# First feed-forward product of six blocks as one Strassen level over 64-row, 128-column products

## The chip, the cores and the metric

The kernel runs on one core of a Trainium2 chip. A core has a matrix engine (TensorE, in the profile PE, with its weight loads shown apart as PEld), a vector engine (VectorE, DVE), an activation engine (ScalarE, ACT), a general engine (GpSimd, POOL) and a queue that issues transfers (SyncE, SP). Each works through its own instructions in their written order and waits on semaphores where it needs another's result. Matrix products end in PSUM, eight banks of 128 partitions x 512 words of 32 bits; everything else stands in SBUF, 128 partitions wide. The metric is the time of one execution on the device, in microseconds (us).

## What is computed

One transformer block on 2048 tokens of 576 features, all inputs in bfloat16. A is linear attention with 32 heads, B the feed-forward part with 4608 hidden features:

```python
mod = (silu(c) @ w_mod).reshape(c.shape[0], 6, 1, -1)
sa, ca, ga, sb, cb, gb = (mod[:, i].copy() for i in range(6))
h = _layernorm(x, axis=-1) * (1 + ca) + sa
x = x + ga * _A_ref(h, A_wqkv, A_w_phi, A_wo)
h = _layernorm(x, axis=-1) * (1 + cb) + sb
x = x + gb * _B_ref(h, B_w1, B_w2)

def _B_ref(x, w1, w2):
    h = jnp.einsum('bsd,df->bsf', x, w1)
    h = jnp.maximum(h, 0)
    return jnp.einsum('bsf,fd->bsd', h, w2)
```

The change is in the first product of B, x @ w1 followed by the maximum with 0.

## The kernel before

**Stages.** The 2048 tokens are 16 tiles of 128 (`NT`), the feed-forward part works on pairs of tiles, eight blocks (`NB`). A first phase, to about 92 us, loads everything, works out the modulation vectors and the keys, values and queries, and sums the key-value matrix. Its order is written out by hand, word by word, in `ORDER`; every word calls one entry of `JOBS`. Some words matter here: `sK` sums exponentials (VectorE, `sums`, L283, into `Rk`), `rK` inverts the sums by a logarithm and an exponential (ScalarE, `k_r`, L300 and L301, into `rk`), `pA` scales them (GpSimd, L594, into `Ak`), `pM` forms a ratio (GpSimd, L599, into `rat`) and multiplies with it (L290). `vE` scales the values with `Ak` (VectorE, L304). `ga` and `gb` are two gate rows: they leave PSUM as quarters into `gt` (`row_e`, L366), go to a buffer in DRAM (`row_w`, L369, one DMA each, `gatd<-gt`) and come back spread over all partitions (`row_r`, L372). `wo` scales the output weights with the first gate row (GpSimd, L632), `xp` scales two tiles of x (GpSimd, L507). Each of `gt`, `Rk`, `rk`, `Ak`, `rat`, `sc`, `mask`, `epsr` and `zero` is an SBUF tile of its own.

**Blocks.** After that, `l1` and `l2` run in turn for each block. `l1(b)` is the first product: the 256 tokens of the block are the moving operand, a 64 x 128 piece of w1 the stationary one. Features come in nine chunks of 64 (`NS`), hidden features in 36 groups of 128. The layout puts the lower half of the hidden features in partitions 0 to 63 and the upper half in 64 to 127, and h2 holds the features in both halves, so two matmuls (`hf` 0 and 1) of 64 rows and 256 columns work in the two halves of the array at the same time. `l1` has nine units `u` of two groups each; a unit fills two banks, and `relu` empties them with two ScalarE instructions (L691 and L692) and one or two of VectorE (L693, and L708 in every third unit) into A11, U3, A12, A22 and U2 in fp16.

`l2(b)` is the second product, by a Strassen scheme of seven products already (Winograd's form): `prod` runs 18 matmuls of 128 x 288 each (L730), with results in banks X, Y and Z, and `fin` adds gates and the residual (VectorE L715 or L717, GpSimd L718 and L719, with `yt` as buffer). The hooks `in_l1` and `in_l2` place the work for later tiles among the matmuls: residual and second layernorm of the next block in `in_l1` (`add_res` L412, `bn` L239 and L240, `ln2_rs` L415 and L416, `ln2_apply` L421, a DMA transpose into h2 at L402) and one query tile in units 5 and 6 (`q_next`: VectorE sums L283, GpSimd L345 and L290, then a DMA transpose into ET at L349); the attention of later tiles (`attend`, L390 with L397 and L398), its transposes (`o_turn`) and the scaling of h2 (`h_scale`, L827) in `in_l2`. `project` (L798 and L805, banks 6, 7, 0 and 1) follows `l2` for blocks 1 to 6, so before the first products of blocks 2 to 7, but not before block 8's.

What the program's engines wait for is put in by the tile framework: it orders any two accesses to the same SBUF or PSUM region of which one writes. The order of the instructions on each engine is the written one (`manual_schedule`).

```python
pe.matmul(PS[:, 2 * u + hf, n * 256 + o:n * 256 + o + w], lhsT=w1[b0:b0 + 64, c, j * P:(j + 1) * P],
          rhs=hb[b0:b0 + 64, c, o:o + w], start=(n == 0 and c == 0 and tile != 0), stop=False,
          skip_group_check=True)
```

Of the kernel before, what the change touches and what calls it, by code (L numbers as in the profile page):

```python
# [60 lines left out]

@with_exitstack
def tile_block(ctx, tc, a, out):
# [51 lines left out]
    mask = small([P, KVW], BF16, "mask")  # L115
    epsr = small([1, KVW + P], BF16, "epsr")
# [18 lines left out]
    sc = small([P, 4, NX], BF16, "sc")  # L135
    Rk = small([P, 4, 2 * H], FP32, "Rk")
    rk = small([P, 4, 2 * H], FP32, "rk")
    Ak = small([P, 4, H], FP32, "Ak")
    rat = small([P, 4, H], FP32, "rat")
# [8 lines left out]
    gt = small([P, 2, D // 4], BF16, "gt")  # L148
# [4 lines left out]
    zero = small([P, 512], BF16, "zero")  # L153
# [56 lines left out]
    load(sp, epsr[:], "epsr")  # L210
# [12 lines left out]
    load(sp, mask[:], "mask")  # L223

    pool.memset(zero[:], 0.0)
# [3 lines left out]
    pool.memset(sc[:], 0.0)  # L229
# [6 lines left out]
    def bn(n, t):  # L236
        s = st[:, t % 4]
        for hf in range(2):
            dve.bn_stats(out=s[:, hf, :], in_=x_sb[:, t, hf * HD:(hf + 1) * HD])  # L239
        dve.bn_aggr(out=mv[:, n, t, :], in_=s)  # L240
# [106 lines left out]

    def q_turn(u):
        sp.dma_start_transpose(ET[:, u % NET], eq(u).rearrange("p (c f) -> p c f", f=P))  # L349
# [24 lines left out]
    def num_mm(t, pr):  # L374
        seen = set()
        parts = []
        for c in range(9):
            h0, h1 = KVC[c]
            if h0 < 16 <= h1:
                parts += [(c, h0, 15), (c, 16, h1)]  # L380
            else:
                parts.append((c, h0, h1))
        for i, (c, h0, h1) in enumerate(parts):
            k = h0 // 16
            b = h0 % 16 * VW
            n = (h1 - h0 + 1) * VW
            kk, o, _ = kvcols(c)
            o += KVN[0] * kk + (h0 - KVC[c][0]) * VW
            last = i + 1 == len(parts) or parts[i + 1][1] // 16 != k
            pe.matmul(pr[:, k, b:b + n], lhsT=ET[:, t % NET, c, :], rhs=kvz[:, o:o + n],  # L390
                      start=k not in seen, stop=last, skip_group_check=True)
            seen.add(k)
# [16 lines left out]

    def add_res(t, pr):  # L410
        x = v2(x_sb[:, t, :])
        dve.tensor_tensor(out=x, in0=x, in1=pr[:, :, 0:HD], op=ALU.add)  # L412
# [5 lines left out]
    def ln2_apply(t):  # L418

        def cols(o, i):  # L420
            dve.tensor_scalar(out=o, in0=i, scalar1=mv[:, 1, t, 0:1], scalar2=rs2[:, t, 0:1],  # L421
                              op0=ALU.subtract, op1=ALU.mult)
        o = xn[:, t % 2, :].rearrange("p (c d f) -> p c d f", d=2, f=64)
        for d in range(2):
            cols(o[:, :, d, :], x_sb[:, t, :].rearrange("p (c f) -> p c f", f=64))
# [21 lines left out]
    w1 = carve(R1, 0, (NS, DFF // 2))  # L447
# [224 lines left out]
    def l1_mm(js, u, hb, tile=None):  # L672
# [6 lines left out]
        for n, c in order:  # L679
            j = js[n]  # L680
            for hf in range(2):
                b0 = 64 * hf
                pe.matmul(PS[:, 2 * u + hf, n * 256 + o:n * 256 + o + w], lhsT=w1[b0:b0 + 64, c, j * P:(j + 1) * P],  # L683
                          rhs=hb[b0:b0 + 64, c, o:o + w], start=(n == 0 and c == 0 and tile != 0), stop=False,
                          skip_group_check=True)
# [23 lines left out]

    def fin(t, k, bank, s, eng=pool):  # L710
# [8 lines left out]
        eng.tensor_tensor(out=x_sb[:, t, c], in0=y, in1=x_sb[:, t, c], op=ALU.add)  # L719

    def l2(b, hooks):
# [31 lines left out]
        if b + 1 == NB:  # L753
            dve.tensor_tensor(out=yl, in0=PS[:, Z, 0:HD], in1=SS[:, 1, :], op=ALU.add)
            pool.tensor_tensor(out=yl, in0=yl, in1=gb_row[:, HD:D], op=ALU.mult)
            pool.tensor_tensor(out=yl, in0=yl, in1=x_sb[:, t, HD:D], op=ALU.add)
        prod(X, A22, T4, al)
        fin(t + 1, 0, X, None, dve if b + 1 == NB else pool)
        sp.dma_start(outf[(t + 1) * P:(t + 2) * P, :], x_sb[:, t + 1, :])
        if b + 1 < NB:  # L760
            prod(Z, A12, B22, al)
            fin(t, 1, Z, 1)
            sp.dma_start(outf[t * P:(t + 1) * P, :], x_sb[:, t, :])
            return
        rows = slice(t * P, (t + 1) * P)
        sp.dma_start(outf[rows, 0:HD], x_sb[:, t, 0:HD])
        for i in range(2):
# [3 lines left out]
            dve.tensor_tensor(out=x_sb[:, t, g], in0=PS[:, i, c], in1=yl[:, c], op=ALU.add)  # L771
        sp.dma_start(outf[rows, HD:D], x_sb[:, t, HD:D])
# [58 lines left out]
    def b0_l1(u):  # L831
        if u < 2:
# [22 lines left out]

    def in_l1(b):
        t = 2 * b + 2

        def hook(u):
# [8 lines left out]
            if b + 1 == NB and u in (1, 3, 5):  # L868
                j = slice(3 * (u - 1), 3 * (u - 1) + 6)
                dve.tensor_tensor(out=B22g[:, j, :], in0=B22[:, j, :],  # L870
                                  in1=gb_row[:, HD:D].unsqueeze(1).to_broadcast([P, 6, HD]), op=ALU.mult)
            if u in (5, 6):
                q_next(min(t + u - 3, NT))
        return hook

    def in_l2(b):
        t = 2 * b + 2

        def hook(pos):
# [5 lines left out]
            if t < NT and pos in ((8, 10, 12) if b == 0 else (1, 3, 5)):  # L885
                h_scale(b + 1, (pos - 8 if b == 0 else pos) // 2)
            if t + 2 < NT and pos in (2, 4):
# [4 lines left out]

    for b in range(NB):
        l1(b, (2, 0, 2, 0, 1, 3, 1, 3, 2) if b == 0 else (2, 1, 0, 3, 2, 1, 0, 3, 2), in_l1(b) if b else b0_l1)
# [9 lines left out]
def _layout(inputs):  # L904
# [72 lines left out]
    w1 = g["B_w1"].reshape(D // 64, 64, 2, DFF // 2)  # L977
    o["w1"] = flat(w1.transpose(2, 1, 0, 3).reshape(P, D // 64, DFF // 2))
# [22 lines left out]
```

## Time and profile before

| | us |
|---|---|
| runs shown | 384.81, 385.29, 385.29 |
| median | 385.29 |
| profiled execution | 384.81 |
| its span (first to last instruction) | 383.04 |
| first phase, to the first matmul of block 1's first product (L683) | 91.6 |
| period of block 3, first product to the next one's | 36.29 |
| of it first product, L683 | 17.68 |
| of it second product, with attention | 16.29 |
| of it projection, L798 and L805 | 2.31 |

The page gives, for one execution, the busy time of each engine, then the chain of work that ended last, followed back from the last instruction; then groups of equal instructions with their line, what they write and read (`out<-in`), the shape, the count, and, behind the first bar, busy time in us and the mean of one in ns. Two TensorE instructions that run at the same time in two halves of the array count once in the busy time. Views by stretch give the length of a stretch and each engine's busy time in it, with the count of instructions in brackets. In a timeline a row is a start in us, a length in us, and the instruction.

### The profile page before, as it was taken

How to read it: one execution, taken by the hardware profiler on the slowest of the kernel's cores; microseconds unless marked ns; L12 is line 12 of the kernel's file. 1: busy time of each engine (PE TensorE's matmuls, PEld its weight loads, DVE VectorE, ACT ScalarE, POOL GpSimd, SP SyncE). 2: the span in 40 equal slices, each digit the busy share in tenths (PEclk: the TensorE clock that was granted, in tenths of full speed). 3: DMA queues.
4: the chain of work that ended last, by engine and by line, in shares of the span. 5: the costliest groups of instructions: out<-in, count | busy, mean ns of one | idle time of the engine just before them, and what ended most of it. 6: DMA issues, size and time to landing. Idle time of an engine off the chain costs nothing.

```text
span 383.0 us, 11398 instructions
## 1 busy us (share of the span) xinstructions
PE 377.9 (99%) x4901; PEld 312.6 (82%) x4901; DVE 241.4 (63%) x440; ACT 186.1 (49%) x449; POOL 122.5 (32%) x194
## 2 busy tenths in 40 slices
PE   8999999999999999999999999999999999999996
PEld 5877788888878888788878887887788888878875
DVE  2899998789989387438734971686277536423442
ACT  2689997689433356315712570346045505622410
POOL 2078899841202302331141133122302230042023
PEclk9999999999999999999999999999999999999999
DMA  7995799888904046203410461073216203001000
GB/s 298 421 417 222 247 406 346 161 221 291 175 20 96 33 48 127 50 33 85 107 34 33 109 95 36 19 126 87 27 31 102 47 31 48 19 0 35 2 2 31
DMA packets 56276, 45.16 MB, mean 118 GB/s; under 512 B 46625, under 2 KB 49314, under 8 KB 55458
## 3 DMA queue, kind: packets, MB, share of 16 engines
q1 hardware_dynamic: 55938, 44.25, 42.4%
q8 instruction: 38, 0.62, 0.7%
q10 hardware_dynamic: 288, 0.19, 0.2%
q14 instruction: 12, 0.10, 0.1%
HBM read 27.38 MB, written 5.90 MB: 87 GB/s over the span
## 4 chain that ended last, share of the span: by engine, by line
PE 82%; DMA 6%; issue 4%; ACT 3%; DVE 2%; POOL 1%; SPq 0%; DVEq 0%; POOLq 0%
PE PS L683 32%; PE PS L730 31%; PE PS L273 10%; PE PS L798 3%; DMA x_sb<-in_xk_dram 2%; DMA RE<-RT 2%; ACT RT L278 2%; DMA R<-in_wkT_dram 2%; PE PS L390 2%; PE PS L323 1%; DVE Rk L283 1%; PE PS L407 1%; PE PS L770 1%; DVE st L239 1%; PE PS L805 1%
## 5 line engine op out<-in xcount | busy, mean ns | idle before, releaser
L683 PE MATMUL PS<-h,R 64*128 64x256 bf16 (+1 forms) x2628 | 143.2, 268 | 0.0
L683 PEld LDWEIGHTS <-R 64*128 64x128 bf16 x2628 | 126.3, 94 | 15.7 <-issue 0.5
L730 PEld LDWEIGHTS <-RH 128*128 128x128 f16 x846 | 81.7, 98 | 21.9 <-issue 1.7
L691 ACT ACTIVATE RH<-PS 128x256 f16<-128x256 f32 x72 | 27.7, 385 | 126.6 <-PE PS L683 126.6
L730 PE MATMUL PS<-R,RH 128*128 128x288 bf16 (+1 forms) x558 | 73.2, 286 | 0.0
L718 POOL TENSOR_TENSOR yt<-yt,gb_row 128x288 f32<-128x288 f32 x23 | 24.9, 1081 | 137.2 <-DVE yt L717 137.2
L693 DVE SCALAR_TENSOR_TENSOR RH<-PS,RH 128x256 f16<-128x256 f32 x72 | 29.5, 416 | 37.5 <-ACT RH L691 37.3
L278 ACT ACTIVATE RT<-PS,rs 128x576 bf16<-128x576 f32 x64 | 42.8, 746 | 2.2 <-PE PS L273 1.8
L692 ACT ACTIVATE RH<-PS 128x512 f16<-128x512 f32 x72 | 42.8, 594 | 0.0
L717 DVE TENSOR_TENSOR yt<-PS,RS 128x288 f32<-128x288 f32 x23 | 10.5, 457 | 46.9 <-PE PS L730 46.8
L730 PE MATMUL PS<-RT,RH 128*128 128x288 f16 x288 | 37.9, 286 | 0.0
L345 POOL TENSOR_TENSOR ratq<-Rq,rq 128x32 f32<-128x32 f32 x16 | 4.7, 296 | 88.5 <-DVE rq L342 88.5
L827 ACT ACTIVATE h<-h,mod 128x256 bf16<-128x256 bf16 x63 | 32.8, 590 | 0.0
L273 PE MATMUL PS<-RH,R 116*128 116x288 bf16 x240 | 32.5, 286 | 0.2 <-DVE RH L520 0.2
L273 PE MATMUL PS<-RH,RT 116*128 116x288 bf16 x240 | 31.9, 286 | 0.1
L239 DVE BATCH_NORM_STATS2 st<-x_sb 128x6 f32<-128x288 bf16 x64 | 25.8, 444 | 3.3 <-DMA x_sb<-in_xk_dram 3.2
L273 PEld LDWEIGHTS <-R 116*128 116x128 bf16 x240 | 22.7, 98 | 6.1 <-issue 0.6
L273 PEld LDWEIGHTS <-RT 116*128 116x128 bf16 x240 | 22.9, 98 | 5.8 <-issue 0.3
L734 ACT ACTIVATE RS<-PS 128x288 f32<-128x288 f32 x24 | 9.8, 410 | 34.2 <-PE PS L730 34.2
L719 POOL TENSOR_TENSOR x_sb<-yt,x_sb 128x288 bf16<-128x288 f32 x30 | 21.9, 729 | 6.3 <-DVE yt L715 4.5
L283 DVE TENSOR_REDUCE Rk<-RT 128x64 f32<-128x1152 bf16 x16 | 21.3, 1337 | 0.9 <-ACT RT L278 0.7
L283 DVE TENSOR_REDUCE Rq<-RT 128x64 f32<-128x1152 bf16 x16 | 21.5, 1343 | 0.2 <-DMA RT<-eqd 0.2
(117 smaller groups left out, 415.1 us busy)
## 6 DMA issues: line engine op xcount, KB each, us to landing
R<-in_w_dram SPq DMA_DIRECT2D x4, 1152.0 KB, 8.4
eqd<-RT SPq DMA_DIRECT2D x12, 288.0 KB, 2.1
RT<-eqd SPq DMA_DIRECT2D x12, 288.0 KB, 3.4
R<-in_w2b_dram SPq DMA_DIRECT2D x2, 1296.0 KB, 8.1
R<-in_w2a_dram SPq DMA_DIRECT2D x3, 864.0 KB
out_dram<-x_sb SPq DMA_DIRECT2D x15, 144.0 KB, 1.7
RT<-in_xT_dram SPq DMA_DIRECT2D x2, 640.0 KB
x_sb<-in_xk_dram SPq DMA_DIRECT2D x3, 288.0 KB, 7.7
```

Source lines behind the costliest of these rows:

```text
L239: dve.bn_stats(out=s[:, hf, :], in_=x_sb[:, t, hf * HD:(hf + 1) * HD])
L273: pe.matmul(pr[:, k, 0:HD], lhsT=xt(t, ck), rhs=w[0:R, ck, k * HD:(k + 1) * HD], start=(ck == 0), stop=(ck == NC - 1))
L278: act.activation(out=E.rearrange("p (b h s e) -> p b h s e", b=2, s=2, e=DH)[:, :, :, s, :], in_=pr[:, :, 0:HD].rearrange("p b (h e) -> p ...
L283: dve.tensor_reduce(out=Rr, in_=E.rearrange("p (c e) -> p c e", e=DH), axis=AXX, op=ALU.add)
L683: pe.matmul(PS[:, 2 * u + hf, n * 256 + o:n * 256 + o + w], lhsT=w1[b0:b0 + 64, c, j * P:(j + 1) * P], rhs=hb[b0:b0 + 64, c, o:o + w], sta ...
L691: act.activation(out=A11[:, j, :], in_=lo[:, :, 0, :], func=ACT.Relu)
L692: act.activation(out=A2[:, j, :, :], in_=PS[:, 2 * u + 1, :].rearrange("p (n s f) -> p n s f", n=2, s=2), func=ACT.Relu)
L693: dve.scalar_tensor_tensor(out=U3[:, j, :], in0=lo[:, :, 1, :], scalar=0.0, in1=A11[:, j, :], op0=ALU.max, op1=ALU.subtract)
L718: pool.tensor_tensor(out=y, in0=y, in1=gb_row[:, c], op=ALU.mult)
L719: eng.tensor_tensor(out=x_sb[:, t, c], in0=y, in1=x_sb[:, t, c], op=ALU.add)
L730: pe.matmul(PS[:, bank, 0:HD], lhsT=am[:, j, :], rhs=bm[:, j, :], start=first and j == 0, stop=(j % 9 == 8), skip_group_check=True)
L827: act.activation(out=o, in_=o, func=ACT.Identity, scale=mod(1, c), bias=mod(0, c))
```

## The change

Blocks 1 and 2 keep `l1`. Blocks 3 to 8 (`b >= BS`, BS = 2) use `l1_seven`. There, 16 of the 18 groups in each half of the hidden features, and eight of the nine feature chunks, are multiplied by one Strassen level: two halves of the features (chunks 0 to 3 and 4 to 7), two halves of the hidden features and the two token tiles of the block make 2 x 2 x 2 products of blocks, of which the scheme needs seven (M1 to M7). The last chunk (r11, r12, r21, r22) and the first two groups (`rawlo`, `rawhi`) are multiplied plainly, the latter in 256 columns as before. Every other matmul has 64 rows, 128 stationary columns and 128 moving columns. The groups are four sets `g` of four.

`SEVEN` writes out the order, banks included. A word with a bar, such as `M1_0|M5_0`, is a step of four matmuls of 128 columns (two of 256) on each side, interleaved, one side in each half of the rows. The other words are the evacuations, which also recombine: A copies one bank into another (ScalarE, PSUM to PSUM) so that different products can be added on both, d copies M5 to SBUF, B and C add d and write PSUM (VectorE), k11 to k22 apply the maximum (ScalarE), U2 forms differences and sums in fp16 (VectorE). `bg` calls the hook that carries residual and layernorm of the next block.

Sums of weights stay resident: w21, w22, w12 and w8 are loaded a second time into SBUF that has become free (`w1_more`) and combined with the first copy (`w1_sum`, VectorE and in part GpSimd) during blocks 1 and 2. Sums of features are formed per block (`t_feat`, four VectorE instructions of 512 columns, late in `in_l2`). To make room, x tiles 8 to 15 leave SBUF after their statistics and are loaded again later (`xs`), ET keeps two slots from tile 8 on (`eslot`), the buffers of d lie in `yt` and `RS`, and nine small tiles of the first phase become columns of one tile, `early`, whose first 4096 columns take w12 later. `q_next` moves from the first product to positions 6 and 8 of the second one (block 2 has both), and `h_scale` from positions 1, 3 and 5 to 2, 4 and 6 from block 3 on. A position is nine matmuls of `prod`.

```diff
+SEVEN = """
+bank:X0=2 bank:Q0=3 bank:Y0=3 bank:Z0=4 bank:W0=3 bank:X1=7 bank:Q1=4 bank:Y1=5 bank:Z1=1 bank:W1=4 bank:X2=3
+bank:Q2=1 bank:Y2=2 bank:Z2=6 bank:W2=7 bank:X3=0 bank:Q3=5 bank:Y3=6 bank:Z3=5 bank:W3=4 bank:rawlo=6 bank:rawhi=5
+M1_0|M5_0 M1_0|M5_0 bg0 M1_0|M5_0 M1_0|M5_0 M5_1|rawhi bg1 M5_1|rawhi d_0 M5_1|rawhi M5_1|rawhi rawlo|rawhi bg2 A_0
+rawlo|rawhi rawlo|rawhi --|rawhi d_1 M6_0|rawhi bg3 M6_0|M1_1 bg4 M6_0|M1_1 M6_0|M1_1 raw1 rawlo|M1_1 rawlo|M2_0 B_0
...
-    mask = small([P, KVW], BF16, "mask")
-    epsr = small([1, KVW + P], BF16, "epsr")
+    early = small([P, 4384], BF16, "early")
+    mask = carve(early, 0, (KVW,))
+    epsr = early[0:1, KVW:2 * KVW + P]
+    zero = carve(early, 2 * KVW + P, (512,))
+    sc = carve(early, 2160, (4, NX))
+    gt = carve(early, 2560, (2, D // 4))
+    Rk, rk = (carve(early, 2848 + 512 * i, (512,)).bitcast(FP32).rearrange("p (a b) -> p a b", a=4) for i in range(2))
+    Ak, rat = (carve(early, 3872 + 256 * i, (256,)).bitcast(FP32).rearrange("p (a b) -> p a b", a=4) for i in range(2))
...
-    Rk = small([P, 4, 2 * H], FP32, "Rk")
-    rk = small([P, 4, 2 * H], FP32, "rk")
-    Ak = small([P, 4, H], FP32, "Ak")
-    rat = small([P, 4, H], FP32, "rat")
...
-    gt = small([P, 2, D // 4], BF16, "gt")
...
+    def w1_sum(k, gp, eng=dve, a=0, n=2048):
+        v = [slot(x, gp)[:, a:a + n] for x in (0, 1, 2, 3, 3, 3, 6, 7)]
+        f = [x.bitcast(FP16) for x in v]
+        o, p, q, op = ((f[6], v[0], v[6], ALU.subtract), (f[7], v[7], f[6], ALU.subtract),
+                       (f[1], v[1], f[7], ALU.subtract), (f[2], v[2], v[3], ALU.add))[k]
+        eng.tensor_tensor(out=o, in0=p, in1=q, op=op)
...
+    TF = carve(RE.bitcast(FP16), 2 * 9 * P, (4, 4, P))
+    DD = (yt.rearrange("p a b -> p (a b)")[:, 0:512], RS[:, 0:1024].bitcast(FP32))
...
+        def quarter(w):
...
+            for s in range(4):
+                i, c = (s, 0) if rest else (k, s)
+                x = hb[r, 8, f * P:f * P + P] if rest else f[r, c, :]
+                yield
+                pe.matmul(PS[:, bank_of[BK[n] + str(g)], i * P:(i + 1) * P], lhsT=w[r, (4 * c + i) * P:(4 * c + i + 1) * P],
+                          rhs=x, start=(n in ("M1", "M5") and i == 0 and c == 0), stop=False, skip_group_check=True)
...
+            if n == "A":
+                act.activation(out=bk["Y"], in_=bk["X"], func=ACT.Copy)
+            elif n == "d":
+                act.activation(out=d, in_=bk["Q"], func=ACT.Copy)
+            elif n == "B":
+                dve.tensor_tensor(out=bk["Z"], in0=bk["X"], in1=d, op=ALU.add)
+            elif n == "C":
+                dve.tensor_tensor(out=bk["W"], in0=bk["X"], in1=d, op=ALU.add)
+            elif n == "U2":
+                dve.tensor_tensor(out=U3[:, j, :], in0=U3[:, j, :], in1=A11[:, j, :], op=ALU.subtract)
+                dve.tensor_tensor(out=U2[:, j, :], in0=U3[:, j, :], in1=A22[:, j, :], op=ALU.add)
+            else:
+                o = {"k11": A11, "k12": U3, "k21": A12, "k22": A22}[n][:, j, :]
+                act.activation(out=o, in_=v[{"k11": "Y", "k12": "Z", "k21": "X", "k22": "W"}[n]], func=ACT.Relu)
...
+    SUM_L1 = {(BS - 1, 7): ((2, 0),), (BS - 1, 8): ((3, 0),)}
+    SUM_L1.update({(BS - 1, u): ((1, u // 4, pool, 512 * (u % 4), 512),) for u in range(7)})
+    SUM_L1[BS - 1, 7] += ((1, 1, pool, 1536, 512),)
+    SUM_L2 = {(BS - 1, 7): (2, 1), (BS - 1, 12): (3, 1), (BS - 2, 11): (0, 0), (BS - 2, 13): (0, 1)}
+    MORE_L1 = {(0, 7): (0, 0), (0, 8): (0, 1)}
+    MORE_L2 = {(0, 1): (1, 0), (0, 7): (1, 1), (0, 9): (3, 0), (0, 10): (3, 1), (BS - 1, 10): (2, 0), (BS - 1, 13): (2, 1)}
...
+            if t < NT and b + 1 >= BS and pos in (9, 11):
+                for k in range(2):
+                    t_feat(b + 1, pos - 9 + k)
...
+            if b + 1 >= BS and pos in (6, 8):
+                q_next(min(2 * b + 6 + (pos - 6) // 2, NT))
...
+        if b < BS:
+            l1(b, (2, 0, 2, 0, 1, 3, 1, 3, 2) if b == 0 else (2, 1, 0, 3, 2, 1, 0, 3, 2), in_l1(b) if b else b0_l1)
+        else:
+            l1_seven(b, in_seven(b))
```

## The prediction

> **What bounds the kernel now.** I read the page first (busy shares, chain that ended last), then the chain in order of time, then TensorE's groups by shape, the sums by stretch, and last the timeline around 37 to 47 us.
>
> ```profile
> PE 377.9 (99%) x4901; PEld 312.6 (82%) x4901; DVE 241.4 (63%) x440; ACT 186.1 (49%) x449; POOL 122.5 (32%) x194
> ...
> PE 82%; DMA 6%; issue 4%; ACT 3%; DVE 2%; POOL 1%; SPq 0%; DVEq 0%; POOLq 0%
> ```
>
> TensorE is busy all the time and is the chain. The chain in order of time says from when:
>
> ```profile
> 52.17 1.77 ACT RT L512 x5
> 53.94 0.36 issue
> 54.29 1.38 ACT RT L278 x2
> ...
> 55.72 2.65 PE PS L273 x20
> ...
> 204.48 17.68 PE PS L683 x324
> 222.16 2.31 PE PS L730 x18
> ```
>
> From 42.9 to 55.7 us ScalarE carries it (exponentials, logarithms, row statistics), from 55.7 TensorE, and then every block's first product is one unbroken piece of 17.68 us: 162 pairs, 109.1 ns a pair, the two of a pair in the two halves of the rows at once.
>
> ```profile
> L683 PE MATMUL PS<-h,R 64*128 64x256 bf16 x2556 | 141.2, 269 | 0.0
> L683 PE MATMUL PS<-h,R 64*128 64x128 bf16 x72 | 2.2, 216 | 0.0
> ```
>
> The second line is the shape that the change uses: block 1's first unit runs 36 pairs of 128 columns, each with its own weight load. Its union, 2.2 us, holds the drain of the last one; the trace's starts lie 55.7 ns apart from pair to pair. (The chain has 4.08 us for these 36 and 18 pairs of 256, which leaves 58.8: the bound above, 0.8 a block.)
>
> ```profile
> 42.80:55.70 12.90, 12.77 (x125) 10.35 (x124) 11.99 (x21) 12.53 (x31) 11.11 (x25) 1.00 1.00 413
> 168.19:185.88 17.69, 17.69 (x326) 15.60 (x322) 13.54 (x26) 7.74 (x20) 2.83 (x4) 1.00 0.33 78
> ```
>
> The columns are length, then busy time of TensorE, its weight loads, VectorE, ScalarE and GpSimd. In the first stretch four engines are all but full: what is lost there is not won back. In block 3's first product VectorE and ScalarE have 4.1 and 9.9 us to spare.
>
> **The change, part by part.**
>
> *1. Products, a gain.* A changed block has 512 matmuls of 128 columns and 36 of 256 instead of 324 of 256, in 74 written steps of two sides; two steps have one side only. 256 pairs x 55.7 ns + 18 x 109.1 ns + half of two lone steps (2 x 4 x 55.7 / 2) = 14.26 + 1.96 + 0.22 = 16.45 us against 17.68: 1.23 a block, 7.4 in six. Weight loads are one per matmul as before. The 36 pairs cover only 2 us, so a slower pace in the long run is rival C.
>
> *2. Evacuation, hidden with little to spare.* ScalarE gets 24 instructions of 512 columns (L692: 594 ns long, the next starts 0.48 later): 11.5, with two raw ones 0.8 and four for the second layernorm 1.0: 13.3 of 16.45 us, was 7.74. VectorE gets 8 additions from PSUM into PSUM. L717 takes 0.457 for 288 columns and L412 0.751 for 576, so 0.69 for 512, and two L412 end in 1.42, so 0.61 each: 4.9. Its 8 subtractions and additions of fp16 go by L708 and L738 (0.56 for 768, 1.36 for 2304): 0.43 and a wake-up, 3.7. Raw 0.8, residual 1.4, statistics 1.9, normalization 2.1: 14.8 of 16.45. Whether it hides is a matter of the banks. Group 0 as example: its M5 is ready after four steps, 0.89, and ScalarE wakes 0.2 after a matmul (so in all L691 rows); the copy d 1.1 to 1.7; the copy A, which writes the same bank, 1.7 to 2.35; TensorE wakes 0.05 after; M6, which adds onto A's source, comes up after the 11.5 steps in front of it at 2.56. Spare: 0.2. Walking all 22 waits of a block so, six have 0.05 to 0.2 to spare and none is late. No row shows VectorE or ScalarE writing PSUM; with 0.06 more on each such write the walk loses 0.15, with 0.06 more on each VectorE instruction about 1.0; below, nothing can be gained. I take 0.15 in each of blocks 3 to 7, +0.75.
>
> *3. Block 8, a small loss.* Before it no projection lies between the products. The first M5 uses bank 3, which VectorE reads for the block before: that read ends at 347.25, 0.57 after L683 starts at 346.68; with the wake-up 0.62. GpSimd's two steps on the row buffer that the copy d now reuses end at 348.86, 2.2 after; so A ends at 3.45, where M6 is due at 2.56 + 0.62: 0.3 more. +0.93.
>
> *4. One tile out of eight, a loss in the first phase.* The gate rows (gt), the sums Rk, their inverses rk, Ak and rat, and sc, mask, epsr and zero become columns of one tile, `early`. The built program's waits show what this does: the DMA that stores a gate row takes every 32nd partition, and it is now ordered against all of Rk, rk, Ak and rat. It waits for the last of VectorE's sums and GpSimd's rat before it, and the next sum, logarithm, Ak and rat wait for it to land. Neither wait is there before.
>
> ```profile
> 37.73 0.51 SPq L369 DMA_DIRECT2D gatd<-gt  x1
> ...
> 38.93 0.27 POOL L599 TENSOR_TENSOR rat<-Rk,rk 128x32 f32<-128x32 f32 x1
> 39.00 1.34 DVE L283 TENSOR_REDUCE Rk<-RT 128x64 f32<-128x1152 bf16 x1
> ...
> 39.34 0.34 SPq L372 DMA_DIRECT2D ga_row<-gatd  x1
> ...
> 42.76 0.52 SPq L369 DMA_DIRECT2D gatd<-gt  x1
> 42.82 1.30 DVE L283 TENSOR_REDUCE Rk<-RT 128x64 f32<-128x1152 bf16 x1
> ...
> 43.88 1.28 POOL L632 TENSOR_TENSOR wo_sb<-wo_sb,ga_row 128x576 bf16<-128x576 bf16 x1 [1.16 <-DMA ga_row<-gatd]
> ...
> 45.61 0.27 POOL L599 TENSOR_TENSOR rat<-Rk,rk 128x32 f32<-128x32 f32 x1
> ...
> 45.96 0.27 ACT L300 ACTIVATE rk<-Rk 128x64 f32<-128x64 f32 x1
> ```
>
> The first store goes out when the sum of 39.00 ends, at 40.35 (was 37.73), and lands 1.6 later, at 41.95 (39.34 less 37.73, since L372 waits for it). The rat of 38.93 then starts at 42.0. Behind it on GpSimd stand L290 1.17 and L507 2.33, to 45.8; L632, which needs the gate row (read at 42.0, 4.5 to landing as before): 46.5 to 47.8; and 0.74 up to the end of the next rat: 48.5. Only now goes the second store (was 42.76), landing at 50.1. For that wait the sum of 42.82: +7.3 on VectorE. Behind it stand all further sums, value scalings and statistics, for which ScalarE waits; its logarithm of 45.96 comes at 51.4. VectorE's idle time in the stretch, 12.90 - 11.99 = 0.9, is absorbed: +6.4 at 55.7, and TensorE, 35.86 of 35.90 us busy from there to block 1, passes all of it on. SP's queue stands too: the loads of the feed-forward weights go out up to 6 later, but are needed only at 98. Bounds: 5.5 (ScalarE's own shift) and 8.3 (the second store landing as late after its issue as now, 3.4, by the semaphores' records; then it stood behind the w2b load issued at 39.73).
>
> *5. Sums, loads, moved pieces, nearly nothing.* Eight loads of up to 0.5 MB and eight x tiles ride where the DMA share is below 0.5. VectorE's weight sums (2048 columns, 1.2 us by L738) stand in block 1's second product and block 2, whose chain is TensorE; uncovered, all six (two are shorter) would cost 5.7. GpSimd's eight pieces (512 columns, about 1.0 by L290's 1.17 for 576) come in block 2, where it works 9.6 of 37.5. The transposes of the query tiles there already end late (154.26, and this period is 37.5, not 36.3), so I put +0.3 (0 to 1). From block 2 on they move into the second product, where VectorE works 7.57 of 18.6: hidden, and the attention of the next block then waits for none. In SP's order they now stand ahead of the second transposed attention tile, which has some 3 us to spare before the projection.
>
> Sum: -7.4 + 0.75 + 0.93 + 6.4 + 0.3 = +1.0. The profiled execution (384.81, its span 383.04 and 1.77 around it) becomes 385.8; the median shown is 0.48 above it, so 386.3 against 385.29.
>
> **The rivals.**
> A. The waits in the first phase cost nothing, because the store lands before anybody needs it: -5.4, 379.9, faster. For it: the tile framework might have left those waits satisfied early. Against it: the store stands behind a sum that ends 2.6 later, and the chain there is full on four engines. It decides below a loss of about 4.5.
> B. VectorE becomes the bound of the first product: 30 instructions x 0.06 = 1.8 on 14.8 leaves no room beside the 1.1 or so in which it must wait for products; 17.4 to 17.6 a block, about +1.0 more in five: 391. For it: the spare times of 0.05 to 0.2. Against: every VectorE duration but the write to PSUM has a row.
> C. Weight loads set the pace of the pairs in the long run. A load of 64 rows takes 94 ns by its group; if a half's next matmul had to wait for a whole one, 256 x (94 - 55.7) = 9.8 a block: 445. For it: a 128-column pair has half the time to hide a load in. Against it: the 36 pairs, which hid theirs. The Trainium skill (TensorE: Matmul & The Clock Gate, section "Back-to-back issue gap") gives about 81 ns per matmul of 128 columns in a stream of loads and matmuls; by that an estimated 425.
> D. TensorE slows down in the pause. While ScalarE stands (46.0 to 51.4) TensorE can fill the free banks, two tiles or 2.45, then pauses about 3. At half speed for as long again it would lose up to 1.5: 387.8. In this trace the granted clock is 1.00 in every stretch, and no pause reaches 1 us, so nothing here shows it. The Trainium skill (TensorE: Matmul & The Clock Gate, "Part 1: The HAM clock gate") halves the clock after an idle window of about 3.4 us.
>
> **Chances.** Forecast 0.52, own range 384.5 to 388; A 0.12; B 0.17; C 0.02; D 0.11; 0.06 for mishaps that cost more. The range 383.0 to 391.5 leaves out A, C and a few of the mishaps. A measurement of this kernel can tell 0.2%, 0.77 us. Faster than 384.5: A and 0.06 of the forecast, 0.18. Within: 0.28 of the forecast and 0.02 of others, 0.30. Slower than 386.1: the rest, 0.52.
>
> **What would show it.** The first L683-like piece of block 1 at 98 instead of 91.6, and in the waits VectorE's sum and GpSimd's rat held by the gate row's store. First products of 16.5 to 16.8 in blocks 3 to 7 and 17.4 in block 8, 55.7 ns a pair. Periods of blocks 3 to 6 of 35.1 to 35.2 (now 36.29). I am wrong if block 1 starts before 95, or if TensorE's waits inside a first product add up to over half a microsecond.

## The result and the profile after

The changed kernel takes 389.06 us in the median of four runs (387.98, 389.04, 389.08, 389.12), the kernel before 385.29 in runs beside it (384.81 to 386.19). The ratio is 1.0088, 95% interval 1.0063 to 1.0114: slower. The profiled execution is the fastest of the four, 387.98, its span 386.20 against 383.04 before.

The page, engines and chain, shows the same bound as before with more work around it: TensorE's busy time fell by 4.8, VectorE's rose by 41 and ScalarE's by 35, and VectorE, the transfers and GpSimd now hold 14% of the chain (9% before).

```profile
PE 373.1 (97%) x6245; PEld 317.6 (82%) x6245; DVE 282.5 (73%) x506; ACT 221.0 (57%) x497; POOL 141.1 (37%) x202
...
PE 80%; DVE 5%; DMA 5%; POOL 4%; ACT 2%; issue 2%; SPq 0%; DVEq 0%; POOLq 0%; ACTq 0%
```

Where the span went, from the starts of the eight first products in the two traces (the prediction's terms are in the third column):

| | before | after | difference | predicted |
|---|---|---|---|---|
| first phase, to block 1 | 91.60 | 98.36 | +6.76 | +6.4 |
| block 1, period | 39.72 | 39.72 | 0 | 0 |
| block 2 | 36.71 | 37.39 | +0.68 | +0.3 |
| block 3 | 36.29 | 35.98 | -0.31 | -1.08 |
| block 4 | 36.28 | 34.94 | -1.34 | -1.08 |
| block 5 | 36.40 | 34.94 | -1.46 | -1.08 |
| block 6 | 36.29 | 35.20 | -1.09 | -1.08 |
| block 7 | 33.32 | 31.97 | -1.35 | -1.08 |
| block 8, to the end | 36.43 | 37.70 | +1.27 | -0.30 |
| sum | 383.04 | 386.20 | +3.16 | +1.0 |

In the chain in order of time (start, length, what) the first phase reads as it was walked. The stretch from 42.80 to 55.70, in which four engines were all but full before, is now a relay of two stores and what stands behind each; the same group of TensorE that started at 55.72 starts at 62.48.

```profile
39.61 1.27 DVE early L302
...
40.93 1.55 DMA gatd<-early
...
42.55 4.49 DMA ga_row<-gatd
...
47.10 1.28 POOL wo_sb L689
48.38 0.35 POOL early L651
...
49.13 1.57 DMA gatd<-early
...
50.73 1.35 DVE early L302
...
62.48 2.65 PE PS L292 x20
```

The waits name both sides: VectorE's sum (L302, was L283) and GpSimd's ratio (L656, was L599) stand for the store of the gate row, 7.3 and 3.0 us.

```profile
DVE early L302 <- DMA gatd<-early: 7.3, 1, 7.3
...
POOL early L656 <- DMA gatd<-early: 3.0, 1, 3.0
```

The sums by stretch (length, then busy time of TensorE, weight loads, VectorE, ScalarE and GpSimd, then the granted clock) stand beside the two shown of before. The first is the stretch from 42.80 to where L292 starts again: 19.68 instead of 12.90, every engine has room, and the granted clock is 0.91. The second is block 4's first product: 16.34 (16.43 to the next matmul) instead of 17.69, TensorE never idle.

```profile
42.80:62.48 19.68, 16.13 (x141) 12.30 (x142) 12.18 (x22) 14.61 (x36) 15.30 (x30) 0.91 0.84 314
211.61:227.95 16.34, 16.34 (x550) 16.23 (x544) 13.12 (x27) 12.75 (x27) 0.00 (x0) 1.00 0.27 53
```

So the product does gain, 1.35 a block, and gives back more elsewhere: in the first phase, in blocks 2 and 3 while the sums are made, and in block 8. The experiments take these apart.

### The profile page after: what moved, and what is told of

It is laid out like the page before. It is cut to its first block, busy times and chain, and to the rows that moved or that the text cites. A ratio compares the mean times of both kernels' runs of the same rounds, so it can differ in the third digit from the quotient of the medians.

```text
span 386.2 us, 14289 instructions
## 1 busy us (share of the span) xinstructions
PE 373.1 (97%) x6245; PEld 317.6 (82%) x6245; DVE 282.5 (73%) x506; ACT 221.0 (57%) x497; POOL 141.1 (37%) x202
## 3 DMA queue, kind: packets, MB, share of 16 engines
HBM read 31.97 MB, written 5.90 MB: 98 GB/s over the span
## 4 chain that ended last, share of the span: by engine, by line
PE 80%; DVE 5%; DMA 5%; POOL 4%; ACT 2%; issue 2%; SPq 0%; DVEq 0%; POOLq 0%; ACTq 0%
PE PS L885 28%; PE PS L805 22%; PE PS L292 11%; PE PS L741 7%; PE PS L953 3%; PE PS L788 2%; DMA R<-in_wkT_dram 2%; PE PS L412 1%; DMA early<-in_w_dram 1%; POOL yt L873 1%; POOL x_sb L874 1%; DMA ga_row<-gatd 1%; DVE early L302 1%; PE PS L342 1%; DVE Rq L302 1%
## 5 line engine op out<-in xcount | busy, mean ns | idle before, releaser
L873 POOL TENSOR_TENSOR yt<-yt,gb_row 128x288 f32<-128x288 f32 x23 | 27.5, 1195 | 178.1 <-DVE yt L872 178.1
L805 PEld LDWEIGHTS <-R 64*128 64x128 bf16 (+1 forms) x1824 | 76.7, 94 | 1.4 <-issue 1.1
L805 PE MATMUL PS<-h,R 64*128 64x128 bf16 x1056 | 58.7, 216 | 0.0
L835 ACT ACTIVATE RH<-PS 128x512 f16<-128x512 f32 x96 | 51.9, 601 | 7.1 <-PE PS L805 6.8
L805 PE MATMUL PS<-RE,R 64*128 64x128 f16 x768 | 39.0, 216 | 0.5 <-DVE yt L872 0.5
L825 ACT ACTIVATE yt<-PS 128x512 f32<-128x512 f32 x12 | 7.2, 597 | 52.4 <-PE PS L805 43.7
L741 PE MATMUL PS<-h,R 64*128 64x256 bf16 (+1 forms) x684 | 36.1, 263 | 0.0
L292 PE MATMUL PS<-RH,R 116*128 116x288 bf16 x240 | 33.7, 292 | 1.6 <-ACT RT L297 1.6
L741 PEld LDWEIGHTS <-R 64*128 64x128 bf16 x684 | 31.6, 94 | 3.9 <-issue 0.2
L292 PE MATMUL PS<-RH,RT 116*128 116x288 bf16 x240 | 32.0, 286 | 0.1
L292 PEld LDWEIGHTS <-R 116*128 116x128 bf16 x240 | 23.2, 100 | 8.1 <-issue 2.0
L805 PEld LDWEIGHTS <-w 64*128 64x128 f16 (+1 forms) x480 | 29.0, 94 | 0.0
L292 PEld LDWEIGHTS <-RT 116*128 116x128 bf16 x240 | 23.0, 98 | 5.9 <-issue 0.2
L805 PE MATMUL PS<-RE,w 64*128 64x128 f16 x384 | 25.3, 216 | 1.5 <-ACT PS L823 1.5
```

Source lines behind the costliest of these rows:

```text
L292: pe.matmul(pr[:, k, 0:HD], lhsT=xt(t, ck), rhs=w[0:R, ck, k * HD:(k + 1) * HD], start=(ck == 0), stop=(ck == NC - 1))
L805: pe.matmul(PS[:, bank_of[BK[n] + str(g)], i * P:(i + 1) * P], lhsT=w[r, (4 * c + i) * P:(4 * c + i + 1) * P], rhs=x, start=(n in ("M1", " ...
L835: act.activation(out=o, in_=v[{"k11": "Y", "k12": "Z", "k21": "X", "k22": "W"}[n]], func=ACT.Relu)
L873: pool.tensor_tensor(out=y, in0=y, in1=gb_row[:, c], op=ALU.mult)
```

## The experiments

### 1. The gate rows out of the shared tile

```diff
-    gt = carve(early, 2560, (2, D // 4))
+    gt = carve(w8, 0, (2, D // 4))
```

> The changed kernel with the gate rows (gt) in columns of w8, which is loaded only later, instead of in early; Rk, rk, Ak and rat stay together in early. Theory (the store of a gate row is ordered against all four and holds the first phase): both waits are gone, block 1's first product starts at 91.5 to 92 us instead of 98.4, and the time falls by 6.5 to 7, to about 382. Rival 1 (the first phase is slower through something else that moved into early, such as sc, mask or the sums themselves): the start stays at 97 to 98.5 and the time at 388 to 389. Rival 2 (the time that the first phase gives back is lost again in blocks 2 and 3, where loads and sums compete): the start is early, but block 4 starts no more than 3 earlier than in the changed kernel (211.6).

Measured: 382.98 us (381.05 to 383.20, five runs), ratio to before 0.9932 (0.9911 to 0.9953); block 1 starts at 91.74, the granted clock is 1.00 throughout, and the span of the profiled execution is 6.9 shorter than the changed kernel's (the median 6.1). Block 4 starts at 204.96 instead of 211.45, 6.5 earlier, so blocks 2 and 3 do not take the gain back. One line, which moves 576 bytes a partition to another tile, turns the change from a loss into a gain. The rest of this study builds on this version unless it says otherwise.

### 2. The old kernel with only the shared tile

```diff
-    Rk = small([P, 4, 2 * H], FP32, "Rk")
-    rk = small([P, 4, 2 * H], FP32, "rk")
-    Ak = small([P, 4, H], FP32, "Ak")
-    rat = small([P, 4, H], FP32, "rat")
+    early = small([P, 1824], BF16, "early")
+    gt = carve(early, 0, (2, D // 4))
+    Rk, rk = (carve(early, 288 + 512 * i, (512,)).bitcast(FP32).rearrange("p (a b) -> p a b", a=4) for i in range(2))
+    Ak, rat = (carve(early, 1312 + 256 * i, (256,)).bitcast(FP32).rearrange("p (a b) -> p a b", a=4) for i in range(2))
...
-    gt = small([P, 2, D // 4], BF16, "gt")
```

> The kernel before with nothing changed but that gt, Rk, rk, Ak and rat are columns of one tile. Theory: the same two waits arise, block 1's first product starts at 98 to 98.5 instead of 91.6, the time rises by 6.5 to 7, to about 392. Rival (the waits matter only together with the other changes): less than 2 us.

Measured: 393.61 us (392.60 to 394.35), ratio 1.0207 (1.0182 to 1.0232); block 1 at 99.59, 8.0 after the kernel before. Together with experiment 1 this shows the tile alone to be cause enough. It also costs 1.2 more here than in the changed kernel's profile, although the second store lands 0.57 earlier (50.13 instead of 50.70). The granted clock goes with it: TensorE pauses from 50.17 to 53.40, and from 52.6 to 59.5 the clock is 0.50. That is rival D, which experiment 5 takes up.

### 3. The loads of w12 earlier

```diff
-(BS - 1, 10): (2, 0), (BS - 1, 13): (2, 1)}
+(BS - 1, 3): (2, 0), (BS - 1, 5): (2, 1)}
```

(in the changed kernel's `MORE_L2`, so that the first products of block 3 do not wait for the load)

> The changed kernel with the two loads of w12 issued at positions 3 and 5 of block 2's second product instead of 10 and 13. Theory (in block 3 TensorE waits 0.9 us for w12, since the load stood in SP's queue behind the transposes of the query tiles): that wait at 179.2 is gone and block 3's first product takes 16.4 to 16.6 instead of 17.5; the whole 0.9 shorter. Rival (the load is not late by its place in the queue but slow by competing transfers): block 3's first product stays above 17.2, or block 2's second product gets longer by as much.

Measured: 390.26 us, one run, slower and not faster. Block 3 did nearly what was expected, 35.19 instead of 35.98 (its first product 16.68 instead of 17.47), its wait of 0.89 gone. But block 2 grew from 37.39 to 38.32: the loads go out at 161.07 and 166.08, ahead of the transposes of the queries and of the attention tile in SP's queue, and the projection waits 1.26 for the second of those. What one transfer gained another lost: blocks 2 and 3 together take 73.51 instead of 73.37. Another 1.8 are in the first phase (block 1 at 100.17), which the edit does not touch: the clock again, below.

### 4. The scaling of B22 later in block 8

```diff
-                if k in (2, 4, 6):
-                    scale_b22(k // 2 - 1)
+                if k in (5, 7, 6):
+                    scale_b22((5, 7, 6).index(k))
```

> The changed kernel with the three VectorE instructions that scale B22 in block 8 moved from hooks 2, 4 and 6 to the later hooks 5, 7 and 6. Theory (in block 8 GpSimd's two steps on yt take 1.48 and 1.42 instead of 0.73 each because VectorE's fp16 scaling runs beside them, so d and A come late): the two steps take 0.73 to 0.8 each, TensorE's wait of 1.66 us at 351.7 falls to 0.2 to 0.5, block 8's first product takes 17.4 to 17.8 instead of 18.9. Rival (the two steps are slow for another reason, such as a late start): they stay above 1.2 and the wait above 1.3.

Measured: 387.84 us, one run, and block 8 takes 36.85 instead of 37.70; the first phase, which the edit does not touch, is 0.5 longer (block 1 at 98.87). The timeline of the changed kernel at block 8's start (start, length, engine, line, what; in brackets the idle time before) shows two GpSimd instructions that take 0.73 elsewhere at twice that, while VectorE's scaling runs beside them; the copy d, which reuses `yt`, waits for the second, the copy A follows d in ScalarE's order, and TensorE waits 1.66 for A.

```profile
349.05 2.55 DVE L1015 TENSOR_TENSOR R<-R,gb_row 128x1728 f16<-128x1728 bf16 x2
...
349.21 1.48 POOL L873 TENSOR_TENSOR yt<-yt,gb_row 128x288 f32<-128x288 f32 x1 [1.47 <-DVE yt L872]
...
350.77 1.42 POOL L874 TENSOR_TENSOR x_sb<-yt,x_sb 128x288 bf16<-128x288 f32 x1
...
352.22 0.60 ACT L825 ACTIVATE yt<-PS 128x512 f32<-128x512 f32 x1 [8.72 <-POOL x_sb L874]
352.85 0.58 ACT L823 ACTIVATE PS<-PS 128x512 f32<-128x512 f32 x1
...
353.49 0.21 PE L805 MATMUL PS<-RE,w 64*128 64x128 f16 x1 [1.50 <-ACT PS L823]
```

With the scaling later, in the timeline of experiment 4, both are back to length, and the wait for A is 0.23:

```profile
349.92 0.74 POOL L873 TENSOR_TENSOR yt<-yt,gb_row 128x288 f32<-128x288 f32 x1 [1.47 <-DVE yt L872]
...
350.74 0.73 POOL L874 TENSOR_TENSOR x_sb<-yt,x_sb 128x288 bf16<-128x288 f32 x1
```

The scaling itself then stands before the additions in VectorE's order and makes them late: 0.71 of new waits between 357.6 and 359.1. So 1.43 of the 1.66 come from the doubled GpSimd steps, and the new waits take half of that away again: the first product falls from 18.89 to 18.21 and not to the expected 17.4 to 17.8.

### 5. The pauses filled

```diff
-... gb:0 gbc gbw kv5 Q1:1 K9:0 ...
+... gb:0 gbc gbw Q1:1 Q1 kv5 Q1 K9:0 ...
-V6:0 rK9 ...
+V6:0 V6 V6 rK9 ...
```

> The changed kernel as it is (one tile, gate rows in it), with four projections of the first phase run twice or three times over into their own banks, just ahead of the two places where TensorE stands waiting (41.7 to 44.2 and about 50.4 to 53.9): the result of the repeats is overwritten by the same values, and only the pauses are filled. Theory (rival D, the clock): the half clock of 44.0 to 47.8 us in the changed kernel's profile, and the one of 52 to 60 us in the two other kernels with the same waits, follow from the pauses, and the difference between executions (387.98 to 389.12) comes from where it falls. Then the granted clock is 1.00 in every stretch, block 1 starts at 97.8 to 98.5, and the time is 387.2 to 388.2 in all runs, within 0.5 of each other. Rival: the clock does not cost anything here and the waits alone vary: median 389.0 as before, spread over 1. Second rival: the repeats delay the evacuations behind them: block 1 at 99 or later, 389.5 or more.

Measured: 387.18 us (386.47 to 389.18, nine runs), ratio 1.0045 (1.0028 to 1.0062), against 1.0088 for the changed kernel. The granted clock is 1.00 in every stretch, so without the pauses it is not halved. Block 1 starts at 97.25, 1.1 earlier than in the changed kernel's profile. But this 1.1 does not come from the clock: it is there before VectorE's sum that waits for the second store starts (here called the second sum).

```profile
43.75 2.28 POOL RT L564
46.03 1.23 POOL wo_sb L689
...
49.62 1.35 DVE early L302
```

The chain of the changed kernel, shown above, has that sum at 50.73. The first store lands 0.4 earlier here, and the gate row lands 3.76 after its issue (4.49 in the changed kernel, 4.48 to 4.93 in all profiles but this one), so that GpSimd goes from L564 to L689 without the wait of 0.69 that it had. Whether the repeats have to do with that landing is not shown. From the second sum to block 1 both executions take the same time, and this stretch is where the clock can be priced:

| | second sum | block 1 | between | clock 0.50 in the first phase |
|---|---|---|---|---|
| changed kernel | 50.73 | 98.36 | 47.63 | 44.0 to 47.4 |
| experiment 5 | 49.62 | 97.25 | 47.63 | none |
| experiment 4 | 50.69 | 98.87 | 48.18 | 44.0 to 47.4, 54.2 to 57.6 |
| experiment 3 | 50.68 | 100.17 | 49.49 | 53.3 to 60.1 |
| experiment 2 (old kernel) | 50.16 | 99.59 | 49.43 | 52.6 to 59.5 |

In the changed kernel's profile the half clock cost nothing: ScalarE did wait for a tile then (2.24, to 47.45), but it had the time, for afterwards it stands 1.99 for the second sum. Behind the sum the half clock cost 0.55 for 3.4 us of it and 1.9 for 6.8 (1.8 in experiment 2, if the old kernel too needs 47.63 without it). The clock by stretches, first of the changed kernel, whose pause was from 42.09 to 44.19 (the clock is the first number behind the five brackets):

```profile
43.00:44.00 1.00, 0.00 (x0) 0.00 (x0) 0.39 (x2) 0.98 (x3) 1.00 (x1) 1.00 0.16 50
44.00:45.00 1.00, 0.81 (x10) 0.77 (x11) 0.00 (x0) 0.97 (x4) 1.00 (x2) 0.51 0.89 119
...
47.00:48.00 1.00, 1.00 (x8) 0.73 (x7) 0.00 (x0) 0.55 (x1) 0.90 (x1) 0.79 0.98 415
```

then the chain of experiment 3, where the first pause, 41.62 to 43.71, changed nothing, and the second, 50.36 to 53.93, was followed by 0.50 up to 60.1: 20 matmuls take 4.96 there and 2.45 after.

```profile
53.93 4.96 PE PS L292 x20
...
61.57 2.45 PE PS L292 x20
```

The Trainium skill (TensorE: Matmul & The Clock Gate, "Part 1: The HAM clock gate") says that the clock is halved after an idle window of about 3.4 us and that these windows run freely. The halving agrees with these traces, and so does its dependence on where a pause falls, but shorter pauses were enough: 2.09 in this kernel's profile, 2.10 and 1.88 in experiment 4's.

What was expected and did not come is that all runs would agree within 0.5: they spread over 2.7 at a clock of 0.999 to 1.000, so the clock is not what makes these executions differ. The median did fall, by 1.9, but what of that is the clock's is open: between the two profiled executions none of it is, and the others were not profiled. What makes executions differ is not settled either. In five profiled ones with the same work there (the changed kernel and experiments 1, 4, 5 and 6) block 2 takes 37.04 to 38.25 and block 3 35.39 to 36.59, both together 73.37 to 73.64; so the experiments on the sums, below, are read from the two blocks together.

### 6. Block 8's first d apart

```diff
-            d = DD[g % 2]
+            d = DD[g % 2] if b + 1 < NB or g else flat(wo_sb).bitcast(FP32)[:, 0:512]
```

> The version with the gate rows apart (382.98), and block 8's first copy d written to an unused part of the output weights' tile instead of the row buffer that GpSimd still adds from. Theory: of block 8's two waits (0.63 for bank 3, 1.67 for the copy A behind d) the second goes, since d starts right after M5: A ends 0.6 + 0.6 after the bank's wait, and M6 is due at 2.56 + 0.63. The first product of block 8 falls from 18.89 to 17.1 to 17.3, the time to 381.2 to 381.5. Rival: A waits for another step of the block before (its bank, or ScalarE's own order): 18.5 or more, time 382.6 or more.

Measured: 379.95 us (379.12 to 380.29), ratio 0.9848 (0.9822 to 0.9873). Block 8's first product falls from 18.89 to 17.14; d starts at 344.17 instead of behind GpSimd, whose two steps still take 1.47 and 1.43 but hold up nobody. This is the better cure than experiment 4's. The wait for bank 3 stays at 0.63, as predicted (0.62). Of the 3.0 between the medians of experiments 1 and 6 the edit explains 1.75; the spans of the two profiled executions differ by 1.1 (379.27 and 378.16), since other stretches take 0.65 more, and the rest of the 3.0 is not settled.

### 7. Block 2 without the sums

```diff
-    SUM_L1 = {(BS - 1, 7): ((2, 0),), (BS - 1, 8): ((3, 0),)}
-    SUM_L1.update({(BS - 1, u): ((1, u // 4, pool, 512 * (u % 4), 512),) for u in range(7)})
-    SUM_L1[BS - 1, 7] += ((1, 1, pool, 1536, 512),)
-    SUM_L2 = {(BS - 1, 7): (2, 1), (BS - 1, 12): (3, 1), (BS - 2, 11): (0, 0), (BS - 2, 13): (0, 1)}
+    SUM_L1 = {}
+    SUM_L2 = {(BS - 2, 11): (0, 0), (BS - 2, 13): (0, 1)}
```

> The version with the gate rows apart (span 379.3), without the weight sums that stand in block 2: the eight pieces on GpSimd and four of VectorE's six whole sums are left out, so the later blocks multiply by weights that were not summed. Loads are as they were. Theory: the sums, by standing in front of GpSimd's and VectorE's steps for the next query tiles, make block 2 37.77 instead of 36.71: without them 36.6 to 36.8, span 378.1 to 378.4. Rival: the loads of the weights in SP's queue do it: block 2 stays at 37.5 or more and the 0.46 of waits in block 3's first product stay too.

Measured: span 377.3 (379.06 us, one run). Block 2 takes 36.65 instead of 37.77 and block 3 34.94 instead of 35.73, together 71.59 instead of 73.50: the sums cost 1.9, and even the wait for the load of w12 goes with them, though no load was moved. The timeline of the changed kernel shows one link of it. GpSimd's small step L364, which the next query tile needs, takes 0.26 alone and 1.23 where VectorE's sum L497 runs (153.42 to 154.79); then a sum of VectorE takes 2.18 beside GpSimd's L309.

```profile
150.68 0.26 POOL L364 TENSOR_TENSOR ratq<-Rq,rq 128x32 f32<-128x32 f32 x1 [6.99 <-DVE rq L361]
...
153.67 1.23 POOL L364 TENSOR_TENSOR ratq<-Rq,rq 128x32 f32<-128x32 f32 x1
154.98 1.17 POOL L309 TENSOR_TENSOR RT<-RT,ratq 128x576 bf16<-128x576 bf16 x1
```

```profile
153.42 1.37 DVE L497 TENSOR_TENSOR R<-R,w 128x2048 f16<-128x2048 bf16 x1
...
155.05 2.18 DVE L497 TENSOR_TENSOR R<-R 128x2048 f16<-128x2048 bf16 x1
```

The Trainium skill (SBUF — State Buffer, "SBUF: two separate sides") has GpSimd and VectorE share one pair of ports that the first of two takes for its whole instruction; these lengths agree: GpSimd's step ends 0.11 after VectorE's sum, and the next sum ends 1.08 after GpSimd's L309 (alone such a sum takes 1.2). VectorE's own order has a part too: both sums stand on the chain of work, 1.29 and 2.10 of it, ahead of the last evacuations of block 2's first product. From there it goes on by order: the transpose of the query tile goes out later, what stands behind it in SP's queue too, and at the end of that row the load that block 3 needs.

### 8. The additions B twice

```diff
-                dve.tensor_tensor(out=bk["Z"], in0=bk["X"], in1=d, op=ALU.add)
+                for _ in range(2):
+                    dve.tensor_tensor(out=bk["Z"], in0=bk["X"], in1=d, op=ALU.add)
```

> The version with the gate rows apart (382.98), with each of the four additions B of a changed block done twice (same operands, same result), so 2.8 us more of VectorE in each first product, whose VectorE was busy 13.1 of 16.34. Theory (the walk of the banks: the evacuations hide, but six of 22 waits have 0.2 or less to spare): TensorE waits 2.1 a block, first products of 18.5, +12.8 in six, 395.8. Rival: the spares are wider than the walk has them, since no stall was seen: under 0.5 a block, 383 to 386. Other rival (VectorE is itself the bound as soon as it is full): the same order as the theory, but the loss then equals 2.8 less the idle 3.2, so nearly nothing.

Measured: 393.69 us, one run, span 391.6 against 379.3; undisturbed first products of 18.62 against 16.43. In block 4 TensorE waits four times, 0.40, 0.33, 0.55 and 0.67, 1.95 in all, and by the view of waits, which counts idle time alone, all on the doubled addition (L828 here):

```profile
PE PS L805 <- DVE PS L828: 7.7, 23, 0.5
```

The walk of the banks had 2.1, so it is right about the size: of 0.70 more at one place 0.33 to 0.67 are passed on, while VectorE is busy 15.89 of the 18.62 and so not full. Busy shares alone would have let these 2.8 into the 3.2 that were free.

### 9. All sums on VectorE

```diff
-    SUM_L1 = {(BS - 1, 7): ((2, 0),), (BS - 1, 8): ((3, 0),)}
-    SUM_L1.update({(BS - 1, u): ((1, u // 4, pool, 512 * (u % 4), 512),) for u in range(7)})
-    SUM_L1[BS - 1, 7] += ((1, 1, pool, 1536, 512),)
+    SUM_L1 = {(BS - 1, 0): ((1, 0),), (BS - 1, 6): ((1, 1),), (BS - 1, 7): ((2, 0),), (BS - 1, 8): ((3, 0),)}
```

> The version with the gate rows and block 8's d apart (379.95, span 378.16, blocks 2 and 3 at 38.25 and 35.39), with the eight GpSimd pieces of the weight sums replaced by two whole sums on VectorE in block 2's first product (units 0 and 6). Theory: what the sums cost in blocks 2 and 3 (1.9 by the run without them) comes mainly from GpSimd, where a step for the next query tiles waits while a VectorE fp16 sum runs (0.26 becomes 1.23) and the pieces stand in its queue: with no pieces, block 2 at 36.9 to 37.4 and block 3 at 35.0 to 35.2, 378.4 to 379.0. Rival: VectorE's own steps for the query tiles stand behind the sums there, 2.5 us later now: block 2 stays at 38 or more, 379.7 or more.

Measured: 381.57 us (381.38 to 382.60), ratio 0.9897 (0.9872 to 0.9921), slower than experiment 6 by the median, with intervals that just touch: the rival won. Block 2 takes 38.76, blocks 2 and 3 together 74.77 instead of 73.64. Three sums in a row, 147.29 to 152.35, stand before the last evacuations of block 2's first product in VectorE's order, and TensorE stands idle for 0.93 in the second product until they are done. Taking the pieces off GpSimd gains nothing where VectorE's order pays for them. (Another 0.86 of the span is a wait inside block 6's first product that the profile puts to "issue", that is, to nothing it shows; the edit does not reach there.)

### 10. The sums spread, part of them in block 3

```diff
+    SUM_L1 = {(BS - 1, 0): tuple((1, 0, pool, 512 * i, 512) for i in range(4)), (BS - 1, 8): ((3, 0),)}
+    SUM_L2 = {(BS - 1, 7): (1, 1), (BS - 1, 12): (3, 1), (BS - 2, 11): (0, 0), (BS - 2, 13): (0, 1)}
...
+            if b == BS and k < 2:
+                for i in range(4):
+                    w1_sum(2, k, pool, 512 * i, 512)
```

(in place of the lines that experiment 9 shows with a minus, and of the old `SUM_L2`; the last three lines in `in_seven`)

> The same version, with the sums so spread that block 2 has four GpSimd pieces instead of eight, all before its query steps, and VectorE three whole sums instead of four; the sums of the third kind go to GpSimd in block 3's first product, where it is idle: eight pieces of 1.1 us, 9 us from its start, needed from about 6.5 and 13.5. Theory: block 2 at 36.7 to 37.1; in block 3 VectorE's own fp16 and bf16 steps are held up by GpSimd's pieces, so that evacuations come late by 0.3 to 1.0 there (35.2 to 36.0): 378.0 to 379.2. Rival: the evacuations in block 3 are late by 2 or more, for the additions stand behind held-up steps: 380 or more.

Measured: 378.98 us (378.59 to 379.59), ratio 0.9822 (0.9802 to 0.9842), the best version here, 10 us below the changed kernel. Block 2 takes 37.15, block 3 35.56 with one wait of 0.48, together 72.71 instead of experiment 6's 73.64. By its median it is a microsecond below experiment 6; the two intervals still overlap, so that last step is likely, not certain.

## Why the prediction was right, and where it was off

The sign held, and so did the mechanism of its two largest terms, the products and the first phase. The time was forecast at 386.3, range 383.0 to 391.5, and came to 389.06: the forecast rise of 1.0 became 3.8. The range reached from faster to much slower, so that the time lies in it says little. One of the forecast's own signs of being wrong came true: TensorE's waits inside a first product add up to 0.9 in block 3 and 2.3 in block 8, not to half a microsecond at most. Point by point:

**Products.** 16.45 a block was forecast, 16.43 measured, at 55.7 ns for each pair over the whole product. Rival C (weight loads set the pace) is refuted. The gain is 1.35 and not 1.23, because by the same measure, from the first matmul to the next product's, the product before takes 17.78, not the 17.68 of the chain.

**Evacuation.** 0.15 a block was put in for stalls; there are none in the undisturbed blocks, so five blocks gained 0.75 more than forecast, except where something else came in between. An addition into PSUM takes 0.70 where the walk had 0.69, so the allowance of 0.06 for each such write was not needed, and rival B is refuted for this kernel. VectorE was put at 14.8 and has 13.1 there, because only five of its eight fp16 steps lie inside the product; the eight additions take 5.6, not 4.9. Experiment 8 shows that the spares are nonetheless small.

**First phase.** Forecast +6.4, in the profile +6.76, and the two stores landed at 42.5 and 50.7 where the walk had 41.95 and 50.1. Experiments 1 and 2 show the cause, and the 0.36 more goes with the stores' times. Rival D, at a chance of 0.11, did take place as well: TensorE paused twice, 2.09 and 1.60 (the rival had one pause of about 3), and the clock was halved for 3.4 us. In the profiled execution that cost nothing, in those of experiments 2 to 4 0.55 to 1.9; which it was in the changed kernel's other executions is not known. The forecast treated the rival as an alternative to its own chain, and it is an addition to it.

**Block 8.** This is the step that failed most: +0.93 was forecast, +2.46 is there (18.89 against 16.43). The bank's 0.62 is 0.63, and 0.17 is spread over the product. The other part, "0.3 more" behind GpSimd's two steps, became 1.66, for these were put at their usual 0.73 each and take 1.48 and 1.42 beside VectorE's scaling of B22. That scaling was not priced: before, it started at 349.54, when GpSimd was done (348.86); with `in_seven` two of its three instructions start right behind VectorE's own last step for block 7, at 349.05, with GpSimd's first. Experiments 4 and 6 show it from two sides.

**Sums.** Forecast +0.3 (0 to 1), because everything stood beside TensorE's chain. In the changed kernel it is 0.68 in block 2 and 1.04 in block 3 (35.98 against the undisturbed 34.94); without the sums 1.9 come back in experiment 7. The busy shares did have room. What was missing is that VectorE's sum and GpSimd's step hold each other up, that the sums stand ahead of evacuations in VectorE's own order, and that the step stands at the head of a queue of transfers. The trace of before had the first of these: VectorE's L708 takes 0.56 alone and 1.57 where GpSimd's L290 runs.

```profile
175.06 0.56 DVE L708 TENSOR_TENSOR RT<-RH 128x768 f16<-128x768 f16 x1
...
180.95 1.17 POOL L290 TENSOR_TENSOR RT<-RT,ratq 128x576 bf16<-128x576 bf16 x1
180.96 1.57 DVE L708 TENSOR_TENSOR RT<-RH 128x768 f16<-128x768 f16 x1
```

The claim that from block 2 on the moved query work has time enough was right only where no sums ran beside it.

**The sum.** Against the profiled execution the terms are off by +0.36 in the first phase, +0.38 in block 2, -0.15 in blocks 3 to 7 together and +1.57 in block 8, 2.16 in all. The other 0.60 of the 2.76 between forecast and measurement is that the profiled execution was 1.08 below its median, not 0.48 as before the change. That this is more time at half clock does not fit: the three longer executions were granted 0.995 to 0.996 of the clock, the profiled one 0.994. Where the half clock fell in them is not on record, so the cause stays open.

## What to carry to other kernels

Before small buffers are gathered in one tile, look for the ones that a transfer touches: the order that it is put in with its neighbours can cost more than a product saves. (Here the transfer takes every 32nd partition; that this stride is why it is ordered against columns it does not touch was not tested.) When work is laid beside other work, compare not busy shares but what the pair does to each other's instructions and who stands behind the slower one. A step that is hidden with 0.2 to spare should be treated as a step on the path, and a stall that idles TensorE should be priced with the clock that can follow it, where the next thing waited for is TensorE's.

## What the runs showed of the hardware

- TensorE's granted clock was 0.50 in stretches of 3.41 us (after pauses of 2.09 in the changed kernel and of 2.10 and 1.88 in experiment 4) or 6.83 us (after 3.23 in experiment 2 and 3.57 in experiment 3). Pauses of 2.10, 2.09 and 1.60 (experiments 2 and 3, the changed kernel) were followed by none. With the pauses filled there was none before the last 0.6 us of the span.
- GpSimd and VectorE held each other up in whole instructions: a GpSimd step of 0.26 took 1.23, one of 0.73 took 1.48, a VectorE sum of 1.2 took 2.18, a VectorE step of 0.56 took 1.57.
- Pairs of matmuls with 64 rows and 128 columns, each with its own weight load, kept 55.7 ns a pair for 16.4 us without a break, as for 2 us before the change.
- ScalarE copied 512 columns from PSUM to PSUM in 0.58, and VectorE added 512 columns in PSUM to SBUF data back into PSUM in 0.70.
